# Cached attention decode with a gated feed-forward mix: per-slab normalization and output projection inside the K/V stream, a fourth K slot, and a longer lead of K over V

## Chip, cores, metric

One core of one Trainium2 chip. The metric is device microseconds of one execution. A *span* is the profiled execution from first to last instruction.

The *granted clock* (PEclk) is the share of its full clock at which TensorE ran, as the profile records it. Its values here are 0.5, called the half clock, and 1.0; figures between are means over a stretch.

Engines: TensorE (PE in the profile; its weight loads are PEld), VectorE (DVE), ScalarE (ACT), GpSimd (POOL), and SyncE (SP), which here issues most DMAs.

## The reference, cut to what matters

```python
x = A_x                                          # 2 x 1 x 512
g = sigmoid((x * gate_w).sum(-1, keepdims=True))
# A: decode attention, B=2 batches, 32 heads, 4096 cached keys, head size 128
q = (x @ wq)                                     # 512 -> 32*128
scores = einsum("bhqd,bhkd->bhqk", q, k) * 128 ** -0.5
o = einsum("bhqk,bhkd->bhqd", softmax(scores), v)
a = o.reshape(2, 1, 4096) @ wo                   # 4096 -> 512
# B: relu feed-forward 512 -> 1376 -> 512
b = relu(x @ w1) @ w2
return g * a + (1 - g) * b
```

There are 64 (batch, head) pairs, called slabs here. Each needs 1 MiB of K and 1 MiB of V. The two caches are 134 MB of the 146 MB that its DMAs move.

## The kernel before

SP queues loads into rings: three slots of K, five of V. V of slab t-2 is issued behind K of slab t; this distance is called the lag below. For each slab, TensorE transposes K in 32 blocks of 128x128. DVE and ACT copy the blocks out of PSUM. TensorE then makes the scores (32 matmuls of one column). A maximum over all partitions on POOL, an exponential on ACT and 32 one-column matmuls with V, together called pv, give the unnormalized output.

```python
RK, RV, RKT, NP, NS = 3, 5, 2, 3, 4
# SP
for t in range(NSLAB):
    dma_k(t)                     # waits until TensorE freed slot t % RK
    if t >= 2:
        dma_v(t - 2)             # waits until TensorE freed slot (t-2) % RV
    ...                          # weights at some t
dma_v(NSLAB - 2)
dma_v(NSLAB - 1)
# TensorE
for t in range(NITER):           # NSLAB + 3
    transposes of slab t, groups 0..3
    scores(t - 1)
    transposes of slab t, groups 4..7
    pv(t - 3)                    # unnormalized output, one column of psACC
    ...
```

Everything else of the attention waits for the last pv: the sums of exponentials, the division, the output projection, and the mix with the feed-forward part.

```python
# TensorE, after the loop
emit(psACC[:, ACC_SUMS:...], lhsT=ones_f, rhs=rowsum)         # sums over partitions
for n4 in range(NN4):            # 4
    for h in range(Hq):          # 32: 128 matmuls of 2 columns
        emit(psACC[:, ACC_AT + 2*n4:...], lhsT=wo_sb[:, h, n4*P:(n4+1)*P], rhs=o_sb[:, 2*h:2*h+2], ...)
for n4 in range(NN4):            # back to rows: 8 matmuls with the identity
    emit(psS[0][0:B, ...], lhsT=at_sb[...], rhs=ident)
    emit(psS[1][0:B, ...], lhsT=fT_sb[...], rhs=ident)
# DVE, after the loop: reciprocal 128x64, multiply 128x64, copy, then three operations of 2x512
```

## Time and profile before

| | before |
|---|---|
| time, median of the first 6 runs | 375.23 us (374.73 to 375.87) |
| span of the profiled execution | 373.9 us |
| DMA rate in mid stream | 412 to 415 GB/s at a busy share of 1.01 to 1.02 |
| TensorE busy | 302.1 us |
| last V load landed (trace of completions) | 362.56 us |
| from there to the end of the span | 11.3 us |

Lines of the profile page of the kernel before: TensorE's busy time; granted clock, DMA share and rate in 40 equal slices; the chain that ended last.

```profile
PE 302.1 (81%) x6502; PEld 297.6 (80%) x6502; DVE 193.7 (52%) x402; ACT 167.4 (45%) x386; POOL 23.3 (6%) x71
...
PEclk9997655765965676568865688565858588686665
DMA  8999999999999999999999999999999999999930
GB/s 293 402 367 406 408 417 419 418 418 421 410 405 421 416 419 399 416 419 415 416 401 407 401 420 409 405 422 403 400 422 418 418 420 415 410 402 420 421 135 2
...
DMA 58%; PE 39%; DVE 1%; issue 1%; ACTq 0%; DVEq 0%
```

DMA is at 9 tenths from the second slice to the 38th. TensorE is busy 81% and yet no limit. The next line is from its list of waits (engine, what it was about to do, what it waited for: us in total, times, longest): it still waits for K to land.

```profile
PE psT L344 <- DMA k_ring<-in_A_k_cache_dram: 46.3, 34, 4.6
```

The windows view gives each engine's busy time in chosen stretches, then granted clock, DMA share and GB/s. It shows a hole near the start:

```profile
core 0: us, PE busy (x) PEld busy (x) DVE busy (x) ACT busy (x) POOL busy (x), PEclk, DMA share, GB/s
20.00:22.00 2.00, 2.00 (x22) 2.00 (x20) 1.68 (x3) 1.29 (x3) 0.00 (x0) 1.00 1.07 369
22.00:24.00 2.00, 2.00 (x49) 2.00 (x48) 1.53 (x3) 1.61 (x3) 0.00 (x0) 1.00 0.90 238
24.00:26.00 2.00, 1.79 (x32) 1.58 (x29) 1.88 (x5) 1.37 (x5) 0.38 (x1) 1.00 1.01 426
...
183.00:330.00 147.00, 124.12 (x2640) 122.50 (x2638) 80.70 (x166) 71.40 (x166) 9.47 (x27) 0.69 1.01 412
```

Here is the timeline of the kernel before, from the last pv on (start us, length us, engine, line, operation, out<-in, shapes, count, idle time before it and its releaser):

```profile
362.69 0.99 PE L344 MATMUL psACC<-p_ring,v_ring 128*128 128x1 bf16 x32 [0.81 <-DMA v_ring<-in_A_v_cache_dram]
...
363.55 0.67 PE L344 MATMUL psACC<-rowsum,ones_f 128*128 128x64 f32 x2
364.25 0.56 DVE L322 RECIPROCAL rinv<-psACC 128x64 f32<-128x64 f32 x1 [3.86 <-PE psACC L344]
364.89 0.23 DVE L324 TENSOR_TENSOR o_sb<-psACC,rinv 128x64 bf16<-128x64 f32 x1
...
365.17 3.57 PE L344 MATMUL psACC<-o_sb,wo_sb 128*128 128x2 bf16 x128 [0.96 <-DVE o_sb L324]
368.78 0.17 DVE L328 CAST at_sb<-psACC 128x8 bf16<-128x8 f32 x1 [3.67 <-PE psACC L344]
...
370.05 0.68 DVE L330 COPY f_sb<-psS 2x512 f32<-2x512 f32 x1 [1.10 <-PE psS L344]
370.81 0.68 DVE L332 TENSOR_TENSOR diff_sb<-psS,f_sb 2x512 f32<-2x512 f32 x1
371.58 0.74 DVE L334 SCALAR_TENSOR_TENSOR fin_sb<-diff_sb,g_sb,f_sb 2x512 bf16<-2x512 f32 x1
372.34 0.31 SPq L183 DMA_DIRECT2D out_dram<-fin_sb  x1
```

Each step waits for the one above it, and no K or V moves any more. The last V was issued at 349.17 and landed 13.39 us later. These 11.3 us cannot overlap with the stream as the kernel stands.

### The profile page before, as it was taken

How to read it: one execution, taken by the hardware profiler on the slowest of the kernel's cores; microseconds unless marked ns; L12 is line 12 of the kernel's file. 1: busy time of each engine (PE TensorE's matmuls, PEld its weight loads, DVE VectorE, ACT ScalarE, POOL GpSimd, SP SyncE). 2: the span in 40 equal slices, each digit the busy share in tenths (PEclk: the TensorE clock that was granted, in tenths of full speed). 3: DMA queues.
4: the chain of work that ended last, by engine and by line, in shares of the span. 5: the costliest groups of instructions: out<-in, count | busy, mean ns of one | idle time of the engine just before them, and what ended most of it. 6: DMA issues, size and time to landing. Idle time of an engine off the chain costs nothing.

```text
span 373.9 us, 14183 instructions
## 1 busy us (share of the span) xinstructions
PE 302.1 (81%) x6502; PEld 297.6 (80%) x6502; DVE 193.7 (52%) x402; ACT 167.4 (45%) x386; POOL 23.3 (6%) x71
## 2 busy tenths in 40 slices
PE   0197879879859998799867988689898988897984
PEld 0197879879859998799867978689898988897974
DVE  0085345655645664466544656355656556465532
ACT  1064334544534554355443555354555455454520
POOL 0000000000000000000000000000000000000000
PEclk9997655765965676568865688565858588686665
DMA  8999999999999999999999999999999999999930
GB/s 293 402 367 406 408 417 419 418 418 421 410 405 421 416 419 399 416 419 415 416 401 407 401 420 409 405 422 403 400 422 418 418 420 415 410 402 420 421 135 2
DMA packets 26711, 146.34 MB, mean 391 GB/s; under 512 B 2230, under 2 KB 7708, under 8 KB 10268
## 3 DMA queue, kind: packets, MB, share of 16 engines
q1 hardware_dynamic: 25588, 142.98, 94.2%
q10 hardware_dynamic: 1064, 2.46, 1.7%
q8 instruction: 51, 0.84, 0.9%
q14 instruction: 8, 0.07, 0.0%
HBM read 145.43 MB, written 0.00 MB: 389 GB/s over the span
## 4 chain that ended last, share of the span: by engine, by line
DMA 58%; PE 39%; DVE 1%; issue 1%; ACTq 0%; DVEq 0%
DMA k_ring<-in_A_k_cache_dram 51%; PE psT L344 26%; PE psS L344 7%; PE psACC L344 5%; DMA wq_sb<-in_A_wq_dram 4%; DMA v_ring<-in_A_v_cache_dram 4%; PE psMISC L344 1%; DVE fin_sb L334 0%; DVE kt_ring L268 0%; DVE diff_sb L332 0%; DVE f_sb L330 0%; DVE rinv L322 0%; ACTq L190 0%; ACTq L192 0%; DVE o_sb L324 0%
## 5 line engine op out<-in xcount | busy, mean ns | idle before, releaser
L268 DVE CAST kt_ring<-psT 128x512 bf16<-128x512 f32 x256 | 172.8, 690 | 123.7 <-PE psT L344 121.7
L344 PE MATMUL psT<-ident,k_ring 128*128 128x128 bf16 x2048 | 198.5, 275 | 46.9 <-DMA k_ring<-in_A_k_cache_dram 46.3
L203 ACT CAST kt_ring<-psT 128x512 bf16<-128x512 f32 x256 | 145.4, 586 | 183.5 <-PE psT L344 182.6
L344 PEld LDWEIGHTS psT<-ident,k_ring 128*128 128x128 bf16 x2048 | 172.4, 127 | 50.2 <-DMA k_ring<-in_A_k_cache_dram 49.7
L344 PE MATMUL psACC<-p_ring,v_ring 128*128 128x1 bf16 x2048 | 63.5, 165 | 1.8 <-issue 1.0
L344 PEld LDWEIGHTS psACC<-p_ring,v_ring 128*128 128x128 bf16 x2048 | 62.7, 101 | 2.1 <-issue 2.0
L344 PE MATMUL psS<-qT_sb,kt_ring 128*128 128x1 bf16 x2048 | 64.0, 165 | 0.1
L344 PEld LDWEIGHTS psS<-qT_sb,kt_ring 128*128 128x128 bf16 x2048 | 63.7, 102 | 0.2
L240 POOL PARTITION_ALL_REDUCE allmax<-colmax x64 | 22.5, 351 | 324.4 <-DVE colmax L275 324.4
L275 DVE TENSOR_REDUCE colmax<-psS 128x1 f32<-128x32 f32 x64 | 12.3, 192 | 27.9 <-PE psS L344 27.9
L210 ACT ACTIVATE p_ring<-psS,negb 128x32 bf16<-128x32 f32 x64 | 18.6, 290 | 3.6 <-DVE negb L281 1.6
L210 ACT ACTIVATION_READ_ACCUMULATOR p_ring<-psS,negb 128x1 f32 x64 | 12.6, 198 | 0.0
L344 PE MATMUL psMISC<-ident,x_sb 2*128 2x2 bf16 x4 | 0.3, 165 | 13.4 <-POOL ident L234 13.4
L344 PEld LDWEIGHTS psMISC<-ident,x_sb 2*128 2x128 bf16 x4 | 0.2, 101 | 13.4 <-POOL ident L234 13.4
L281 DVE TENSOR_SCALAR negb<-allmax 128x1 f32<-128x1 f32 x64 | 9.2, 144 | 0.5 <-POOL allmax L240 0.5
L344 PE MATMUL psMISC<-xT_sb,wq_sb 128*128 128x2 bf16 x128 | 4.0, 165 | 3.7 <-DMA wq_sb<-in_A_wq_dram 3.7
L344 PEld LDWEIGHTS psMISC<-xT_sb,wq_sb 128*128 128x128 bf16 x128 | 3.7, 104 | 3.8 <-issue 3.8
L344 PEld LDWEIGHTS psACC<-o_sb,wo_sb 128*128 128x128 bf16 x128 | 3.5, 104 | 1.1 <-DVE o_sb L324 1.1
L344 PE MATMUL psACC<-o_sb,wo_sb 128*128 128x2 bf16 x128 | 3.6, 165 | 1.0 <-DVE o_sb L324 1.0
L248 DVE SCALAR_TENSOR_TENSOR gscr<-x_sb,gw_sb 2x512 f32<-2x512 bf16 x1 | 0.7, 680 | 6.8 <-DMA gw_sb<-in_gate_w_dram 6.8
L253 DVE CAST xT_sb<-psMISC 128x8 bf16<-128x8 f32 x1 | 0.2, 167 | 6.2 <-PE psMISC L344 6.2
L196 ACT ACT_TABLE_LOAD x1 | 1.3, 1283 | 3.1 <-issue 3.1
(32 smaller groups left out, 15.2 us busy)
## 6 DMA issues: line engine op xcount, KB each, us to landing
k_ring<-in_A_k_cache_dram SPq DMA_DIRECT2D x64, 1024.0 KB, 11.4
v_ring<-in_A_v_cache_dram SPq DMA_DIRECT2D x64, 1024.0 KB, 13.7
wo_sb<-in_A_wo_dram SPq DMA_DIRECT2D x4, 1024.0 KB, 15.8
wq_sb<-in_A_wq_dram SPq DMA_DIRECT2D x3, 1024.0 KB, 14.8
w_sb<-in_B_w_dram ACTq DMA_DIRECT2D x1, 1376.0 KB, 19.9
w_sb<-in_B_w_dram SPq DMA_DIRECT2D x1, 1280.0 KB, 20.4
wq_sb<-in_A_wq_dram ACTq DMA_DIRECT2D x1, 1024.0 KB, 15.3
w_sb<-in_B_w_dram SPq DMA_DIRECT2D x1, 96.0 KB, 21.0
```

The source lines that it names most:

```text
L196: nc.scalar.activation(out=gexp[:, :], in_=gdot[:, :], func=AF.Exp, scale=-1.0).then_inc(sem_gexp, 1)
L203: nc.scalar.copy(out=kt_ring[:, ks, 4 * g:4 * g + 4, :], in_=psT[b][:, :].rearrange("p (a d) -> p a d", d=P),).then_inc(sem_cp[b], 1)
L210: nc.scalar.activation(out=p_ring[:, u % NP, :], in_=psS[u % 2][:, 0:NCH], func=AF.Exp, bias=negb[:, u % NS:u % NS + 1], scale=SCALE, accu ...
L240: nc.gpsimd.partition_all_reduce(allmax[:, u % NS:u % NS + 1], colmax[:, u % NS:u % NS + 1], channels=P, reduce_op=RMAX,).then_inc(sem_all ...
L248: nc.vector.scalar_tensor_tensor(out=gscr[:, :], in0=x_sb[:, :], scalar=1.0, in1=gw_sb[:, :], op0=ALU.mult, op1=ALU.mult, accum_out=gdot[: ...
L253: nc.vector.tensor_copy(out=xT_sb[:, :], in_=psMISC[:, M_XT:M_XT + 2 * KT]).then_inc(sem_xTsb, 1)
L268: nc.vector.tensor_copy(out=kt_ring[:, ks, 4 * g:4 * g + 4, :], in_=psT[b][:, :].rearrange("p (a d) -> p a d", d=P),).then_inc(sem_cp[b], 1)
L275: nc.vector.tensor_reduce(out=colmax[:, u % NS:u % NS + 1], in_=psS[u % 2][:, 0:NCH], axis=AX.X, op=ALU.max).then_inc(sem_rmax, 1)
L281: nc.vector.tensor_scalar_mul(negb[:, u % NS:u % NS + 1], allmax[:, u % NS:u % NS + 1], -SCALE).then_inc(sem_negb, 1)
L344: mm = nc.tensor.matmul(out_ap, lhsT=lhsT, rhs=rhs, start=start, stop=stop)
```

## The change

The intent is to normalize and project each slab as soon as its pv is done, so that little is left at the end, and to prefetch K deeper. The projection of one head becomes a single matmul of 512 columns with a weight from `wo`, called a row or wo row below. The diff, cut and condensed to its core:

```diff
-    RK, RV, RKT, NP, NS = 3, 5, 2, 3, 4
+    RK, RV, RKT, NP, NS = 4, 5, 2, 3, 4
+    LV = 3
@@ SP
-                if t >= 2:
-                    dma_v(t - 2)
+                if t >= LV:
+                    dma_v(t - LV)
@@ POOL: a second all-reduce per slab, for the sum of exponentials
+            def do_sums(u):
+                pool.wait_ge(sem_exp, u + 1)
+                nc.gpsimd.partition_all_reduce(S_sb[:, ...], rowsum[:, ...], channels=P, reduce_op=RADD)
@@ DVE: per slab, after the row maximum
+                dve_recip(t - 3)          # 128x1
+                dve_norm(t - 4)           # o_sb column = psACC column * reciprocal
@@ TensorE: one row of the projection per slab of the second batch
+            def a_rows_mm(h):
+                emit(psEPI[0:B, 0:D], lhsT=o_sb[:, 2*h:2*h+2], rhs=wo_sb[:, h, :], start=(h == 0), stop=(h == Hq-1), ...)
@@ TensorE: the loop (NITER is now NSLAB + 4)
+                if t == 0:
+                    qT_piece(0)           # first q projection between the halves of slab 0's transposes
                 ...
                 pv(t - 3)                 # now also waits for the normalization of the slab before
+                h_a = t - 36
+                if 0 <= h_a < Hq:
+                    a_rows_mm(h_a)
@@ the feed-forward result is made as rows too (11 matmuls of 512 columns) and scaled by 1-g early
-                fT_mms()
+                f_rows_mms()
@@ after the loop: sums, 128 wo matmuls, identity matmuls and five DVE operations go; one DVE operation stays
```

More of the change, by code (lines that the diff above doesn't have):

```diff
@@ L17, in bass_gated_mix__gqa_block_cached__dense_activation_relu__decode_kernel @@
     RMAX = bass.bass_isa.ReduceOp.max
+    RADD = bass.bass_isa.ReduceOp.add
     B, _, D = A_x.shape
@@ L28, in bass_gated_mix__gqa_block_cached__dense_activation_relu__decode_kernel @@
     WLAST = Dff - NJF * P
-    NN4 = D // P
     SCALE = float(Dh) ** -0.5
     GROUPS = NCH // 4
-    RK, RV, RKT, NP, NS = 3, 5, 2, 3, 4
+    NTB = 4
+    RK, RV, RKT, NP, NS = 4, 5, 2, 3, 4
+    LV = 3
     QT_PIECES = 4
@@ L52, in bass_gated_mix__gqa_block_cached__dense_activation_relu__decode_kernel @@
         g_sb = ctx.enter_context(nc.sbuf_tensor("g_sb", [B, 1], f32))
+        omg = ctx.enter_context(nc.sbuf_tensor("omg", [B, 1], f32))
         ident = ctx.enter_context(nc.sbuf_tensor("ident", [P, P], bf16))
         itmp = ctx.enter_context(nc.sbuf_tensor("itmp", [P, P], bf16))
-        ones_f = ctx.enter_context(nc.sbuf_tensor("ones_f", [P, P], f32))
         xT_sb = ctx.enter_context(nc.sbuf_tensor("xT_sb", [P, 2 * KT], bf16))
         hT_sb = ctx.enter_context(nc.sbuf_tensor("hT_sb", [P, 2 * NJ], bf16))
-        fT_sb = ctx.enter_context(nc.sbuf_tensor("fT_sb", [P, 2 * NN4], bf16))
         qT_sb = ctx.enter_context(nc.sbuf_tensor("qT_sb", [P, 2 * Hq], bf16))
@@ L63, in bass_gated_mix__gqa_block_cached__dense_activation_relu__decode_kernel @@
         negb = ctx.enter_context(nc.sbuf_tensor("negb", [P, NS], f32))
+        S_sb = ctx.enter_context(nc.sbuf_tensor("S_sb", [P, NS], f32))
+        rS_sb = ctx.enter_context(nc.sbuf_tensor("rS_sb", [P, NS], f32))
         rowsum = ctx.enter_context(nc.sbuf_tensor("rowsum", [P, NSLAB], f32))
         o_sb = ctx.enter_context(nc.sbuf_tensor("o_sb", [P, NSLAB], bf16))
-        rinv = ctx.enter_context(nc.sbuf_tensor("rinv", [P, NSLAB], f32))
-        at_sb = ctx.enter_context(nc.sbuf_tensor("at_sb", [P, 2 * NN4], bf16))
         f_sb = ctx.enter_context(nc.sbuf_tensor("f_sb", [B, D], f32))
-        diff_sb = ctx.enter_context(nc.sbuf_tensor("diff_sb", [B, D], f32))
+        pre_sb = ctx.enter_context(nc.sbuf_tensor("pre_sb", [B, D], f32))
         fin_sb = ctx.enter_context(nc.sbuf_tensor("fin_sb", [B, D], bf16))
-        psT = [ctx.enter_context(nc.psum_tensor(f"psT{i}", [P, 512], f32)) for i in range(4)]
+        psT = [ctx.enter_context(nc.psum_tensor(f"psT{i}", [P, 512], f32)) for i in range(NTB)]
         psS = [ctx.enter_context(nc.psum_tensor(f"psS{i}", [P, 512], f32)) for i in range(2)]
@@ L75, in bass_gated_mix__gqa_block_cached__dense_activation_relu__decode_kernel @@
         psMISC = ctx.enter_context(nc.psum_tensor("psMISC", [P, 512], f32))
-        ACC_O, ACC_SUMS, ACC_AT = 0, NSLAB, 2 * NSLAB
-        M_QT, M_XT, M_HT, M_FT = 0, 2 * Hq, 2 * Hq + 2 * KT, 100
+        psEPI = psMISC
+        M_QT, M_XT, M_HT = 0, 2 * Hq, 2 * Hq + 2 * KT
         def sem(name):
@@ L99, in bass_gated_mix__gqa_block_cached__dense_activation_relu__decode_kernel @@
         sem_hTsb = sem("sem_hTsb")
-        sem_fT = sem("sem_fT")
-        sem_fTsb = sem("sem_fTsb")
-        sem_tr = [sem(f"sem_tr{i}") for i in range(4)]
-        sem_cp = [sem(f"sem_cp{i}") for i in range(4)]
+        sem_f = sem("sem_f")
+        sem_fsb = sem("sem_fsb")
+        sem_tr = [sem(f"sem_tr{i}") for i in range(NTB)]
+        sem_cp = [sem(f"sem_cp{i}") for i in range(NTB)]
         sem_scores = sem("sem_scores")
@@ L108, in bass_gated_mix__gqa_block_cached__dense_activation_relu__decode_kernel @@
         sem_exp = sem("sem_exp")
+        sem_S = sem("sem_S")
+        sem_pv = sem("sem_pv")
+        sem_onrm = sem("sem_onrm")
         sem_gdot = sem("sem_gdot")
         sem_gexp = sem("sem_gexp")
-        sem_sums = sem("sem_sums")
-        sem_onrm = sem("sem_onrm")
-        sem_AT = sem("sem_AT")
-        sem_ATsb = sem("sem_ATsb")
-        sem_rows = sem("sem_rows")
+        sem_A = sem("sem_A")
         sem_fin = sem("sem_fin")
@@ L124, in slab_col @@
             return 2 * h + b
-        NITER = NSLAB + 3
+        NITER = NSLAB + 4
         @block.sync
@@ L179, in _ @@
                     dma_wo_piece((t - 16) // 8)
-            dma_v(NSLAB - 2)
-            dma_v(NSLAB - 1)
+            for u in range(NSLAB - LV, NSLAB):
+                dma_v(u)
             sp.wait_ge(sem_fin, 1)
@@ L184, in _, with group_info @@
             sp.wait_ge(sem_out, 16)
+        def group_info(t, g):
+            G = GROUPS * t + g
+            bank = G % NTB
+            k = G // NTB
+            return bank, k
         @block.scalar
@@ L199, in act_copy @@
                 ks = t % RKT
-                b = g % 4
-                n = 2 * t + g // 4 + 1
-                act.wait_ge(sem_tr[b], n)
+                bank, k = group_info(t, g)
+                act.wait_ge(sem_tr[bank], k + 1)
                 nc.scalar.copy(
                     out=kt_ring[:, ks, 4 * g:4 * g + 4, :],
-                    in_=psT[b][:, :].rearrange("p (a d) -> p a d", d=P),
-                ).then_inc(sem_cp[b], 1)
+                    in_=psT[bank][:, :].rearrange("p (a d) -> p a d", d=P),
+                ).then_inc(sem_cp[bank], 1)
             def act_exp(u):
@@ L231, in _ @@
             pool.memset(itmp[:, :], 1.0)
-            pool.memset(ones_f[:, :], 1.0)
             pool.drain()
@@ L237, in _, with do_allmax @@
             ).then_inc(sem_ident, 1)
-            for u in range(NSLAB):
+            def do_allmax(u):
                 pool.wait_ge(sem_rmax, u + 1)
@@ L242, in _ @@
                 ).then_inc(sem_allred, 1)
+            def do_sums(u):
+                pool.wait_ge(sem_exp, u + 1)
+                nc.gpsimd.partition_all_reduce(
+                    S_sb[:, u % NS:u % NS + 1], rowsum[:, slab_col(u):slab_col(u) + 1], channels=P, reduce_op=RADD,
+                ).then_inc(sem_S, 1)
+            for u in range(NSLAB):
+                do_allmax(u)
+                if u >= 1:
+                    do_sums(u - 1)
+            do_sums(NSLAB - 1)
         @block.vector
@@ L253, in _ @@
             nc.vector.tensor_copy(out=xT_sb[:, :], in_=psMISC[:, M_XT:M_XT + 2 * KT]).then_inc(sem_xTsb, 1)
-            dve.wait_ge(sem_qT, 1)
-            nc.vector.tensor_copy(
-                out=qT_sb[:, 0:2 * HEADS_PER_PIECE], in_=psMISC[:, M_QT:M_QT + 2 * HEADS_PER_PIECE]
-            ).then_inc(sem_qTsb, 1)
             dve.wait_ge(sem_gexp, 1)
@@ L261, in _ @@
             dve.reciprocal(g_sb[:, :], g1[:, :])
+            dve.drain()
+            dve.tensor_scalar(omg[:, :], g_sb[:, :], -1.0, 1.0, ALU.mult, ALU.add)
             def dve_copy(t, g):
                 ks = t % RKT
-                b = g % 4
-                n = 2 * t + g // 4 + 1
-                dve.wait_ge(sem_tr[b], n)
+                bank, k = group_info(t, g)
+                dve.wait_ge(sem_tr[bank], k + 1)
                 nc.vector.tensor_copy(
                     out=kt_ring[:, ks, 4 * g:4 * g + 4, :],
-                    in_=psT[b][:, :].rearrange("p (a d) -> p a d", d=P),
-                ).then_inc(sem_cp[b], 1)
+                    in_=psT[bank][:, :].rearrange("p (a d) -> p a d", d=P),
+                ).then_inc(sem_cp[bank], 1)
             def dve_reduce_max(u):
@@ L283, in dve_negb, with dve_recip, dve_norm @@
                 ).then_inc(sem_negb, 1)
+            def dve_recip(u):
+                dve.wait_ge(sem_S, u + 1)
+                dve.reciprocal(rS_sb[:, u % NS:u % NS + 1], S_sb[:, u % NS:u % NS + 1])
+            def dve_norm(u):
+                col = slab_col(u)
+                dve.wait_ge(sem_pv, u + 1)
+                nc.vector.tensor_tensor(
+                    out=o_sb[:, col:col + 1], in0=psACC[:, col:col + 1], in1=rS_sb[:, u % NS:u % NS + 1],
+                    op=ALU.mult,
+                ).then_inc(sem_onrm, 1)
             def dve_qT_copy(pz):
@@ L299, in _ @@
                     dve_reduce_max(u)
+                if t == 0:
+                    dve_qT_copy(0)
+                ur = t - 3
+                if 0 <= ur < NSLAB:
+                    dve_recip(ur)
+                un = t - 4
+                if 0 <= un < NSLAB:
+                    dve_norm(un)
                 if t < NSLAB:
@@ L311, in _ @@
                 if t == 5:
-                    dve.wait_ge(sem_fT, 1)
-                    nc.vector.tensor_copy(out=fT_sb[:, :], in_=psMISC[:, M_FT:M_FT + 2 * NN4]).then_inc(sem_fTsb, 1)
+                    dve.wait_ge(sem_f, 1)
+                    nc.vector.tensor_copy(out=f_sb[:, :], in_=psEPI[0:B, 0:D]).then_inc(sem_fsb, 1)
+                    dve.drain()
+                    dve.tensor_scalar_mul(pre_sb[:, :], f_sb[:, :], omg[:, 0:1])
                 if t == 7:
@@ L319, in _ @@
                     dve_qT_copy(3)
-            dve.wait_ge(sem_sums, 1)
-            dve.reciprocal(rinv[:, :], psACC[:, ACC_SUMS:ACC_SUMS + NSLAB])
-            dve.drain()
-            nc.vector.tensor_tensor(
-                out=o_sb[:, :], in0=psACC[:, ACC_O:ACC_O + NSLAB], in1=rinv[:, :], op=ALU.mult
-            ).then_inc(sem_onrm, 1)
-            dve.wait_ge(sem_AT, 1)
-            nc.vector.tensor_copy(out=at_sb[:, :], in_=psACC[:, ACC_AT:ACC_AT + 2 * NN4]).then_inc(sem_ATsb, 1)
-            dve.wait_ge(sem_rows, 1)
-            dve.tensor_copy(out=f_sb[:, :], in_=psS[1][0:B, 0:D])
-            dve.drain()
-            dve.tensor_tensor(out=diff_sb[:, :], in0=psS[0][0:B, 0:D], in1=f_sb[:, :], op=ALU.subtract)
-            dve.drain()
+            dve.wait_ge(sem_A, 1)
             nc.vector.scalar_tensor_tensor(
-                out=fin_sb[:, :], in0=diff_sb[:, :], scalar=g_sb[:, 0:1], in1=f_sb[:, :],
+                out=fin_sb[:, :], in0=psEPI[0:B, 0:D], scalar=g_sb[:, 0:1], in1=pre_sb[:, :],
                 op0=ALU.mult, op1=ALU.add,
@@ L360, in qT_piece @@
                 pe.wait_ge(sem_wq[pz], 16)
+                if pz == 0:
+                    pe.wait_ge(sem_xTsb, 1)
                 for hh in range(HEADS_PER_PIECE):
@@ L368, in qT_piece @@
                              inc=(sem_qT, 1) if last else None)
-            pe.wait_ge(sem_xTsb, 1)
-            qT_piece(0)
             def transposes(t, g):
-                b, h = slabs[t]
                 ks_in = t % RK
-                bank = g % 4
-                n = 2 * t + g // 4
-                if n > 0:
-                    pe.wait_ge(sem_cp[bank], n)
+                bank, k = group_info(t, g)
+                if k > 0:
+                    pe.wait_ge(sem_cp[bank], k)
                 for i in range(4):
@@ L394, in scores @@
                 if explicit_cp_wait:
-                    for bank in range(4):
-                        pe.wait_ge(sem_cp[bank], 2 * u + 2)
+                    need = [0] * NTB
+                    for g in range(GROUPS):
+                        bank, k = group_info(u, g)
+                        need[bank] = max(need[bank], k + 1)
+                    for bank in range(NTB):
+                        if need[bank] > 0:
+                            pe.wait_ge(sem_cp[bank], need[bank])
                 for c in range(NCH):
@@ L405, in pv @@
                 pe.wait_ge(sem_exp, u + 1)
+                if u >= 1:
+                    pe.wait_ge(sem_onrm, u)
                 pe.wait_ge(sem_v[vs], 16 * (u // RV + 1))
                 for c in range(NCH):
-                    emit(psACC[:, ACC_O + col:ACC_O + col + 1],
+                    emit(psACC[:, col:col + 1],
                          lhsT=v_ring[:, vs, c, :], rhs=p_ring[:, u % NP, c:c + 1],
                          start=(c == 0), stop=(c == NCH - 1),
-                         inc=(sem_vfree[vs], 1) if c == NCH - 1 else None)
+                         inc=(sem_pv, 1) if c == NCH - 1 else None)
+                pending.append((sem_vfree[vs], 1))
             def hT_mms():
@@ L423, in hT_mms, with f_rows_mms @@
                              inc=(sem_hT, 1) if last else None)
-            def fT_mms():
+            def f_rows_mms():
                 pe.wait_ge(sem_w2, 32)
                 pe.wait_ge(sem_hTsb, 1)
-                for n4 in range(NN4):
-                    for j in range(NJ):
-                        w = P if j < NJF else WLAST
-                        last = (n4 == NN4 - 1) and (j == NJ - 1)
-                        emit(psMISC[:, M_FT + 2 * n4:M_FT + 2 * n4 + 2],
-                             lhsT=w2_sb[0:w, j, n4 * P:(n4 + 1) * P], rhs=hT_sb[0:w, 2 * j:2 * j + 2],
-                             start=(j == 0), stop=(j == NJ - 1),
-                             inc=(sem_fT, 1) if last else None)
+                for j in range(NJ):
+                    w = P if j < NJF else WLAST
+                    emit(psEPI[0:B, 0:D],
+                         lhsT=hT_sb[0:w, 2 * j:2 * j + 2], rhs=w2_sb[0:w, j, :],
+                         start=(j == 0), stop=(j == NJ - 1),
+                         inc=(sem_f, 1) if j == NJ - 1 else None)
+            def a_rows_mm(h):
+                pe.wait_ge(sem_onrm, Hkv + h + 1)
+                if h == 0:
+                    pe.wait_ge(sem_fsb, 1)
+                    pe.wait_ge(sem_qTsb, 4)
+                if h % HEADS_PER_PIECE == 0:
+                    pe.wait_ge(sem_wo[h // HEADS_PER_PIECE], 16)
+                emit(psEPI[0:B, 0:D], lhsT=o_sb[:, 2 * h:2 * h + 2], rhs=wo_sb[:, h, :],
+                     start=(h == 0), stop=(h == Hq - 1),
+                     inc=(sem_A, 1) if h == Hq - 1 else None)
             for t in range(NITER):
@@ L444, in _ @@
                     scores(u, explicit_cp_wait=(t >= NSLAB))
+                if t == 0:
+                    qT_piece(0)
                 if t < NSLAB:
@@ L454, in _ @@
                 if t == 4:
-                    fT_mms()
+                    f_rows_mms()
                 if t == 6:
-                    pe.wait_ge(sem_fTsb, 1)
+                    pe.wait_ge(sem_fsb, 1)
                     qT_piece(1)
@@ L464, in _ @@
                     qT_piece(3)
-            pe.wait_ge(sem_exp, NSLAB)
-            emit(psACC[:, ACC_SUMS:ACC_SUMS + NSLAB], lhsT=ones_f[:, :], rhs=rowsum[:, :],
-                 start=True, stop=True, inc=(sem_sums, 1))
-            pe.wait_ge(sem_onrm, 1)
-            for pz in range(QT_PIECES):
-                pe.wait_ge(sem_wo[pz], 16)
-            for n4 in range(NN4):
-                for h in range(Hq):
-                    last = (n4 == NN4 - 1) and (h == Hq - 1)
-                    emit(psACC[:, ACC_AT + 2 * n4:ACC_AT + 2 * n4 + 2],
-                         lhsT=wo_sb[:, h, n4 * P:(n4 + 1) * P], rhs=o_sb[:, 2 * h:2 * h + 2],
-                         start=(h == 0), stop=(h == Hq - 1),
-                         inc=(sem_AT, 1) if last else None)
-            pe.wait_ge(sem_ATsb, 1)
-            pe.wait_ge(sem_fTsb, 1)
-            for n4 in range(NN4):
-                emit(psS[0][0:B, n4 * P:(n4 + 1) * P],
-                     lhsT=at_sb[:, 2 * n4:2 * n4 + 2], rhs=ident[:, :], start=True, stop=True)
-                emit(psS[1][0:B, n4 * P:(n4 + 1) * P],
-                     lhsT=fT_sb[:, 2 * n4:2 * n4 + 2], rhs=ident[:, :], start=True, stop=True,
-                     inc=(sem_rows, 1) if n4 == NN4 - 1 else None)
             assert not pending
```

## The prediction

> **What bounds the kernel now.** DMA. The windows view shows a DMA share of 1.01 to 1.02 and 412 to 415 GB/s from 34 to 352 us; the page's chain gives DMA 58%. TensorE is second: 302.1 us busy of 373.9, and in the list of waits it still waits 46.3 us for k_ring landings, so it keeps up. The stream cannot be shortened by doing less on the engines: bytes and packets are the same before and after.
>
> **Where time is to be had: the two ends.** In the timeline the last V slab was issued at 349.17 and landed 13.39 us later, at 362.56. From there to the end, 11.3 us, nothing streams: pv(63) 0.99, the ones-by-rowsum matmuls 0.67, reciprocal 0.56 and multiply 0.23 on 128x64, 128 wo matmuls 3.57, a cast 0.17, eight identity matmuls about 1, three 2x512 DVE operations of 0.68, 0.68 and 0.74, and about 1.55 from the end of the last one to the end of the span.
>
> **Tail after.** Sums, reciprocals, all but one normalization and all but two wo rows lie inside the stream. From the landing of V63: 0.1 start, pv(63) 1.0, then the wo row of head 30 runs while norm(63) (estimate 0.15, as the cast of 128x8 took 0.17) is done, then head 31's. A 512-column row is estimated from the identity matmuls (16 of 128 columns took 1.89 us at granted clock 0.5): 0.45 us, 0.6 to its end. Final operation 0.74, output 1.55. Sum 4.3 to 4.5 us instead of 11.3: saves 6.9.
>
> **Head.** K3 waited for the release of ring slot 0 until 21.98 us; between 22.5 and 24.0 us the stream fell to 174 to 240 GB/s. With four K slots K3, V0 and the next wq piece are queued before that wait. I estimate 0.3 MB, 0.5 us, gained. Half of the first transposes move ahead of the q projection; that shortens TensorE only.
>
> **What is added, and hidden.** DVE: 64 reciprocals and 64 multiplies, 0.13 to 0.17 each as the 128x1 negb's 0.144, so +18 us to about 212 of 368. POOL: 64 more all-reduces at 0.35 (if add costs as max). TensorE: 32 rows of 512 columns, 8 to 15 us, minus about 5 removed; only in the second half, where the windows view has it 84% busy. Deeper K prefetch covers bursts. The Trainium skill, "TensorE: Matmul & The Clock Gate", Part 1, says that activity releases the half clock; the trace's clock does switch between 0.5 and 1.0 only, so more work should raise the mean (0.699) rather than starve the stream. The later V (lag 3) still lands before its pv: about 2.5 us after its K, with 3 us of work between.
>
> **Sum.** 375.2 - 6.9 - 0.5 = 367.8 us, range 366.0 to 370.2. Faster by over 2% means below 367.7, so it is nearly even: faster 0.48, within 2% 0.50, slower 0.02.
>
> **Signs.** Right if V63 lands at 361.5 to 362.6, 4 to 5 us before the end; no DMA dip at 22.5 to 24; k_ring waits remain, though fewer.
>
> **What would make it wrong.** TensorE falling behind in the second half (k_ring waits vanish); the add all-reduce taking microseconds; drain of uneven DMA engines (205 GB/s from 357 to 360) growing or shrinking.

## The result

The changed kernel takes 368.12 us (median of 8 runs, 367.61 to 368.73). The kernel before takes 375.25 us (16 runs, 374.56 to 375.91). The ratio is 0.981, with a 95% interval from 0.980 to 0.982. Ratios in this document divide the mean of one kernel's fast runs by that of the other's of the same rounds, so they are not quite the ratios of the medians.

The same views of the changed kernel follow. First, its page:

```profile
PE 308.7 (84%) x6363; PEld 291.6 (80%) x6363; DVE 198.6 (54%) x527; ACT 167.3 (46%) x386; POOL 46.1 (13%) x134
...
PEclk9996756766655886558875885559677688595885
DMA  8999999999999999999999999999999999999971
GB/s 297 390 390 412 409 417 416 420 418 421 407 409 421 419 415 398 420 418 417 419 391 419 421 417 410 390 421 421 416 421 419 417 419 416 421 419 419 419 310 66
...
DMA 70%; PE 26%; SPq 2%; issue 1%; DVE 0%; ACTq 0%
...
L251 POOL PARTITION_ALL_REDUCE S_sb<-rowsum x64 | 29.2, 456 | 0.3 <-ACT p_ring L215 0.3
...
L368 PE MATMUL psMISC<-wo_sb,o_sb 128*2 128x512 bf16 x32 | 14.4, 457 | 0.0
```

TensorE's wait for K, and the windows:

```profile
PE psT L368 <- DMA k_ring<-in_A_k_cache_dram: 36.9, 29, 4.2
```

```profile
20.00:22.00 2.00, 1.80 (x30) 1.58 (x28) 1.48 (x3) 1.07 (x2) 0.11 (x1) 1.00 1.11 394
22.00:24.00 2.00, 2.00 (x52) 1.79 (x50) 1.70 (x5) 1.50 (x5) 0.42 (x2) 1.00 0.99 401
24.00:26.00 2.00, 2.00 (x62) 2.00 (x60) 1.22 (x4) 1.33 (x4) 0.57 (x2) 1.00 0.97 397
...
183.00:330.00 147.00, 130.30 (x2681) 121.92 (x2677) 83.66 (x223) 71.49 (x167) 19.82 (x56) 0.72 1.02 415
```

The timeline from the last pv on:

```profile
361.92 0.99 PE L368 MATMUL psACC<-p_ring,v_ring 128*128 128x1 bf16 x32 [0.69 <-DMA v_ring<-in_A_v_cache_dram]
...
362.84 1.01 PE L368 MATMUL psMISC<-wo_sb,o_sb 128*2 128x512 bf16 x2
362.95 0.16 DVE L306 TENSOR_TENSOR o_sb<-psACC,rS_sb 128x1 bf16<-128x1 f32 x1 [2.04 <-PE psACC L368]
...
363.89 0.74 DVE L358 SCALAR_TENSOR_TENSOR fin_sb<-psMISC,g_sb,pre_sb 2x512 bf16<-2x512 f32 x1 [0.78 <-PE psMISC L368]
364.65 0.32 SPq L183 DMA_DIRECT2D out_dram<-fin_sb  x1
```

The last V landed at 361.78 us and the span ended at 366.2. The tail is 4.43 us instead of 11.33, which saves 6.9. The last landing is 0.8 us earlier, and the hole at 22 us is gone (401 GB/s instead of 238). Together that is 7.7 us between the two profiled executions. The medians differ by 7.1, because the two profiled executions lie on opposite sides of their medians.

In mid stream almost nothing changed: from 183 to 330 us the share of DMA is 1.01 before and 1.02 after, at 412 and 415 GB/s.

### The profile page after: what moved, and what is told of

It is laid out like the page before. It is cut to its first block, busy times and chain, and to the rows that moved or that the text cites. A ratio compares the mean times of both kernels' runs of the same rounds, so it can differ in the third digit from the quotient of the medians.

```text
span 366.2 us, 14094 instructions
## 1 busy us (share of the span) xinstructions
PE 308.7 (84%) x6363; PEld 291.6 (80%) x6363; DVE 198.6 (54%) x527; ACT 167.3 (46%) x386; POOL 46.1 (13%) x134
## 4 chain that ended last, share of the span: by engine, by line
DMA 70%; PE 26%; SPq 2%; issue 1%; DVE 0%; ACTq 0%
DMA k_ring<-in_A_k_cache_dram 62%; PE psT L368 18%; PE psS L368 5%; DMA v_ring<-in_A_v_cache_dram 4%; DMA wq_sb<-in_A_wq_dram 3%; PE psACC L368 2%; PE psMISC L368 2%; SPq L151 1%; SPq L134 0%; DVE fin_sb L358 0%; DVE kt_ring L282 0%; SPq L161 0%; ACTq L196 0%; ACTq L198 0%; ACTq L197 0%
## 5 line engine op out<-in xcount | busy, mean ns | idle before, releaser
L368 PE MATMUL psT<-ident,k_ring 128*128 128x128 bf16 x2048 | 194.7, 272 | 37.5 <-DMA k_ring<-in_A_k_cache_dram 36.9
L368 PEld LDWEIGHTS psT<-ident,k_ring 128*128 128x128 bf16 x2048 | 168.2, 125 | 49.0 <-DMA k_ring<-in_A_k_cache_dram 43.8
L251 POOL PARTITION_ALL_REDUCE S_sb<-rowsum x64 | 29.2, 456 | 0.3 <-ACT p_ring L215 0.3
L368 PE MATMUL psMISC<-wo_sb,o_sb 128*2 128x512 bf16 x32 | 14.4, 457 | 0.0
L306 DVE TENSOR_TENSOR o_sb<-psACC,rS_sb 128x1 bf16<-128x1 f32 x64 | 9.2, 143 | 4.0 <-PE psACC L368 4.0
L301 DVE RECIPROCAL rS_sb<-S_sb 128x1 f32<-128x1 f32 x64 | 9.8, 153 | 0.4 <-POOL S_sb L251 0.4
```

The source lines that it names most:

```text
L251: nc.gpsimd.partition_all_reduce(S_sb[:, u % NS:u % NS + 1], rowsum[:, slab_col(u):slab_col(u) + 1], channels=P, reduce_op=RADD,).then_inc ...
L301: dve.reciprocal(rS_sb[:, u % NS:u % NS + 1], S_sb[:, u % NS:u % NS + 1])
L306: nc.vector.tensor_tensor(out=o_sb[:, col:col + 1], in0=psACC[:, col:col + 1], in1=rS_sb[:, u % NS:u % NS + 1], op=ALU.mult,).then_inc(sem ...
L368: mm = nc.tensor.matmul(out_ap, lhsT=lhsT, rhs=rhs, start=start, stop=stop)
```

## Experiments

Two theories stood at the start. The first is the prediction's: the shortened end gives nearly all, and the ring only fills the hole at the head. The rival is that the deeper ring feeds the stream and is worth several microseconds. Twelve kernels ran. Every result was correct. The table is ordered by what was asked. "Gap" is the time from the landing of the last K to that of the last V, and "tail" the time from there to the end of the span. Both are read from the trace's record of completed loads in one profiled execution.

| run | median us (range) | ratio to before | gap us | tail us |
|---|---|---|---|---|
| before | 375.25 (374.56 to 375.91) | | 8.81 | 11.33 |
| changed | 368.12 (367.61 to 368.73) | 0.981 | 10.77 | 4.43 |
| e1 ring and lag alone, on the kernel before | 374.70 (374.60 to 375.08) | 0.9984 | 11.41 | 11.33 |
| e2 ring and lag undone | 369.90 (369.14 to 371.89) | 0.9867 | 7.42 | 9.72 |
| e3 head order undone | 368.26 (368.06 to 368.40) | 0.9811 | 11.17 | 4.43 |
| e7 ring 3, lag 3 | 368.21 (367.76 to 371.43) | 0.9827 | 11.08 | 4.65 |
| e8 ring 4, lag 2 | 369.70 (367.88 to 374.73) | 0.9847 | 7.54 | 8.51 |
| e4 all wo rows at the end | 376.20 (375.29 to 376.83) | 1.0019 | 11.00 | 13.20 |
| e6 wo rows doubled | 368.89 (368.77 to 369.02) | 0.9832 | 10.93 | 5.28 |
| e11 e2 with rows doubled | 369.90 (369.23 to 372.70) | 0.9861 | 8.27 | 6.73 |
| e9 last V split, row first | 367.75 (367.17 to 367.99) | 0.9798 | 10.93 | 4.59 |
| e10 e9 with spare rows | 369.58 (368.92 to 371.21) | 0.9849 | 11.10 | 7.47 |
| e12 e9 with row order mended | 368.10 (367.20 to 370.16) | 0.9819 | 11.11 | 3.89 |
| e5 loads moved between DMA engines | 441.81 (438.42 to 446.30) | 1.1735 | | |

The ranges of e5 and e8 include runs called slow: two of e5, above 446 us, and one of e8, 374.73 us, each over 1.5% above the fastest of its kernel. The ratios leave them out. The 95% intervals of the ratios reach 0.001 to 0.002 to each side, for e2, e7, e8, e11 and e12 0.002 to 0.003, and for e5 0.004.

### e1: the ring and the lag alone, on the kernel before

```diff
-    RK, RV, RKT, NP, NS = 3, 5, 2, 3, 4
+    RK, RV, RKT, NP, NS = 4, 5, 2, 3, 4
-                if t >= 2:
-                    dma_v(t - 2)
+                if t >= 3:
+                    dma_v(t - 3)
```

> The kernel before with four K slots and V issued three slabs behind K, nothing else changed. Theory (the epilogue gives nearly all, the ring only fills the dip at 22 us): 0.3 to 1.0 us faster than before, so 374.3 to 375.0 us, the last V landing at most 1 us earlier, tail after it still 11.3 us. Rival (the deeper ring feeds the stream and is worth several us): 372 us or less.

It took 374.70 us against 375.27 in the same rounds, 0.57 us faster. The tail is unchanged at 11.33 us, and the windows view from 22 to 24 us gives 401 GB/s. So the ring and lag together are worth about half a microsecond on the old kernel. The rival is out.

### e2: the ring and the lag undone in the changed kernel

```diff
-    RK, RV, RKT, NP, NS = 4, 5, 2, 3, 4
-    LV = 3
+    RK, RV, RKT, NP, NS = 3, 5, 2, 3, 4
+    LV = 2
```

> The changed kernel with three K slots and V two slabs behind, as before the change. Theory: loses only the 0.3 to 1.0 us of the head, 368.4 to 369.1 us, tail after the last landing still 4.4 us. Rival (the ring is worth several us): 371 us or more.

Neither theory fits. It lost 1.8 us by the medians, and its runs scatter. In its profiled execution, one of the two slowest at 371.89 us, the last V landed at 360.44 us, earlier than in the changed kernel, but the tail was 9.72 us. The windows view of that run:

```profile
340.00:345.00 5.00, 5.00 (x93) 4.55 (x92) 2.74 (x8) 2.62 (x6) 0.71 (x2) 0.50 1.01 421
345.00:350.00 5.00, 5.00 (x96) 4.95 (x94) 3.15 (x8) 2.60 (x6) 0.71 (x2) 0.50 1.02 421
350.00:355.00 5.00, 5.00 (x77) 4.60 (x77) 2.93 (x7) 1.90 (x5) 0.71 (x2) 0.50 1.01 415
355.00:360.00 5.00, 5.00 (x88) 4.55 (x86) 2.58 (x8) 2.16 (x6) 0.71 (x2) 0.50 0.57 236
```

TensorE is busy 5.00 of every 5.00 us, at granted clock 0.50. Its timeline shows the first transposes of the last slab and the last pv:

```profile
356.13 1.89 PE L368 MATMUL psT<-ident,k_ring 128*128 128x128 bf16 x16
...
365.84 1.01 PE L368 MATMUL psACC<-p_ring,v_ring 128*128 128x1 bf16 x32
```

K of that slab had landed at 353.02 us. TensorE came to it 3.1 us late, then needed 10.7 us (356.13 to 366.85) for all that lies behind the last K. The last V had been in place for 5 us when its product began. So in this run TensorE set the end, not DMA.

### e3: the order at the head undone

```diff
+            qT_piece(0)
             for t in range(NITER):
 ...
-                if t == 0:
-                    qT_piece(0)
```

> The changed kernel with the first q projection ahead of all transposes again. Theory: TensorE is not the limit in the head, so the same within 0.3 us, 367.8 to 368.5 us. Rival (starting the transposes earlier releases slot 0 earlier and is part of the gain): 0.5 us or more slower.

It took 368.26 us with the same tail of 4.43 us. Moving the first q projection behind half of the transposes is worth nothing that these runs resolve.

### e7 and e8: which of ring and lag

e7 sets `RK` to 3 and keeps `LV` at 3. e8 keeps `RK` at 4 and sets `LV` to 2.

> The changed kernel with three K slots but V still three slabs behind K. Undoing both slots and lag cost 1.8 us, more than the head explains; in that trace TensorE was busy without a gap from 340 us on at granted clock 0.50 and finished behind the stream. Lag theory (with lag 3 the last K has four V loads behind it instead of three, so TensorE gets 2.5 us more for its last slabs): within 0.6 us of the changed kernel, 367.8 to 368.7 us. Ring theory (the fourth slot lets K run ahead of a slow TensorE): 369.3 us or more.

> The changed kernel with four K slots but V two slabs behind K. Lag theory: 369.3 us or more, the last V landing earlier than TensorE is ready for it. Ring theory: within 0.6 us of the changed kernel, 367.8 to 368.7 us.

e7 is level with the changed kernel by its median (368.21 us). The intervals of the two ratios overlap (0.9803 to 0.9852 against 0.980 to 0.982), so no cost of the missing fourth slot is shown. e8 is as late as e2 (369.70), and its runs scatter as widely. It differs from the changed kernel in the lag alone, and its interval (0.9826 to 0.9869) lies apart. So the lag costs time, and the number of slots is not shown to. (Set against each other, the intervals of e7 and e8 overlap.) The table's gaps show why. With lag 2, three V loads follow the last K, and the last V lands 7.4 to 8.8 us after it. With lag 3 there are four, and the gap is 10.8 to 11.4 us. Behind the last K, TensorE has its slab, the scores of two slabs, four more pv and the last rows to do. Where the gap is shorter than that work, the last V waits for TensorE. The timeline of e8's profiled execution (370.72 us) shows the first transposes of the last slab and the last pv:

```profile
355.76 1.07 PE L368 MATMUL psT<-ident,k_ring 128*128 128x128 bf16 x16
...
364.67 1.01 PE L368 MATMUL psACC<-p_ring,v_ring 128*128 128x1 bf16 x32
```

That stretch is 8.9 us, more than the gap of 7.54, although the granted clock was 1.00 from 350 to 360 us (0.57 in the mean from 360 to 365). TensorE had also come to the last K 2.8 us after its landing (352.94). Both together make the last pv 4.2 us late (the last V landed at 360.48). One of e7's six runs took 371.43 us. No trace shows why, but lag 3 is no assurance that every execution is in time.

On the old kernel the gap of 8.81 us was just enough: its last pv had waited 0.81 us for V. The change put rows and waits into that stretch, and also lengthened the stretch.

### e4: all wo rows behind the loop

```diff
-                h_a = t - 36
-                if 0 <= h_a < Hq:
-                    a_rows_mm(h_a)
 ...
+            for h in range(Hq):
+                a_rows_mm(h)
```

> The changed kernel with all 32 wo rows behind the loop instead of one per slab. Theory (the gain is that the projection is hidden, not that it is cheaper): 30 more rows of 0.43 us at the half clock after the last landing, about 12.5 us more, 379 to 381 us, slower than before the change. If the clock rises while they run, 0.22 us each from some point on: 375 to 379. Rival (the row form itself is cheaper than 128 narrow matmuls): 371 us or less.

It took 376.20 us, so the whole gain was gone. The timeline of the end:

```profile
362.76 9.79 PE L368 MATMUL psMISC<-wo_sb,o_sb 128*2 128x512 bf16 x32
...
372.59 0.74 DVE L358 SCALAR_TENSOR_TENSOR fin_sb<-psMISC,g_sb,pre_sb 2x512 bf16<-2x512 f32 x1 [9.56 <-PE psMISC L368]
```

The row form takes 9.79 us for what 128 narrow matmuls did in 3.57. It pays only because 30 of its 32 rows hide behind DMA. My first figure, 379 to 381 us, was too high because the granted clock rose while the rows ran: it was 0.50 up to 366 us and 1.00 from 369 us on. The second alternative held.

### e6: every wo row computed twice

```diff
-                     start=(h == 0), stop=(h == Hq - 1), inc=...)
+                     start=(h == 0), stop=False)
+                emit(psEPI[0:B, 0:D], lhsT=o_sb[:, 2*h:2*h+2], rhs=wo_sb[:, h, :], start=False, stop=(h == Hq - 1), inc=...)
 ...
-                out=fin_sb[:, :], in0=psEPI[0:B, 0:D], scalar=g_sb[:, 0:1], ...
+                out=fin_sb[:, :], in0=psEPI[0:B, 0:D], scalar=gh_sb[:, 0:1], ...   # gh = g / 2
```

> The changed kernel with every wo row computed twice into the same sum and the gate halved, so the result is right; adds 14.4 us of TensorE work to the second half and one row, 0.43 us, to the end. Prediction's view (ample slack in TensorE): 368.3 to 368.8 us. Thin slack (0.45 us per slab on top of 84% busy plus the first row leaves nothing at the half clock): 369.5 to 373 us, and the last V waits for TensorE.

It took 368.89 us, 0.77 more than the changed kernel. That is 0.09 us above the range of the prediction's view, and well below that of thin slack. The tail grew by 0.85 us (5.28 against 4.43), since two rows more lie in it, so the tail accounts for all of it. The 30 rows in the stream cost nothing. This line of its page shows what happened:

```profile
PE 302.3 (82%) x6395; PEld 276.3 (75%) x6395; DVE 196.0 (53%) x528; ACT 166.6 (45%) x386; POOL 46.1 (13%) x134
```

TensorE did more work and was busy for less time, 302.3 us instead of 308.7. Its mean granted clock was 0.79 instead of 0.72 in the profiled executions. The Trainium skill, "TensorE: Matmul & The Clock Gate", Part 1, says that the default state is the half clock and that activity releases it. This pair of runs agrees in direction. e2 does not fit so simply: there TensorE had no gap for 20 us and stayed at 0.50.

### e11: does a higher clock cure e2?

This is e2 with the rows doubled as in e6.

> Three K slots and lag 2 as in the run with the ring undone (369.9 us), and every wo row doubled as in the doubled-row run (368.9 us with ring and lag in place). Clock theory (the ring undone is slow because TensorE ends the stream at the half clock, and more work lifts the clock): 368.7 to 369.3 us, faster than with less work, and a narrower range than 369.1 to 371.9. Work theory (TensorE is late because there is too much to do): 371 us or more.

It took 369.90 us, the same as e2, so both theories missed. In the profiled execution the clock was up:

```profile
340.00:345.00 5.00, 4.09 (x106) 3.57 (x102) 2.91 (x9) 2.55 (x7) 0.71 (x2) 1.00 1.02 423
345.00:350.00 5.00, 4.12 (x107) 3.59 (x104) 2.94 (x9) 2.58 (x7) 0.71 (x2) 1.00 1.02 423
350.00:355.00 5.00, 4.09 (x106) 3.57 (x103) 2.91 (x9) 2.56 (x7) 0.71 (x2) 1.00 0.93 387
```

TensorE had gaps and met the last K as it landed, at 353.34 us. Its last pv still began at 363.17, 1.6 us after the last V (361.60). Even with the clock mostly up, then, the work behind the last K, with its doubled rows, took longer than the gap of 8.3 us. How much of e2's lateness is due to its slow clock is not separated by this, because the doubled rows also add work behind the last K. But e8 was late with no doubled rows and with the clock at 1.00 for the ten us before 360. What e2, e8 and e11 share is the short gap. In e2 and e8, over half of the lateness was there when the last K landed (3.1 and 2.8 us): TensorE still had work of earlier slabs to do.

### e9, e12, e10: can the remaining tail be cut?

e9 cuts the last V load into four by chunks, with a semaphore each, and puts each wo row ahead of the slab's pv:

```diff
+            for i in range(NPC):                      # 4
+                sp.dma_start(v_ring[:, s, c0:c1, :], src[:, c0:c1, :]).then_inc(sem_vlast[i], 16)
 ...
+                    if u == NSLAB - 1 and c % (NCH // NPC) == 0:
+                        pe.wait_ge(sem_vlast[c // (NCH // NPC)], 16)
```

> The changed kernel with the last V load cut into four by chunks, each with its own semaphore, so that three quarters of the last product run before the last landing, and with the wo row of a slab put ahead of that slab's product instead of behind it. Theory (the 4.4 us after the last landing are a chain of which the product, 1.0 us, and the row of head 30, about 0.2 us beyond the normalization, can be taken out): 0.7 to 1.0 us faster, 367.1 to 367.4 us. Rival (smaller packets on the slow DMA engines delay the landing by as much): within 0.3 us of 368.1.

It took 367.75 us, with a ratio to before of 0.9798 (0.9784 to 0.9811). That lies between the two ranges. It is 0.37 us less than the changed kernel, and the intervals overlap, so it is not shown to be better. In its trace the last pv began at 362.06 us, later than the last landing at 361.68. The order may be the reason, since a row ahead of a pv waited about 0.25 us for the normalization just before it. e12 asks whether it is.

e12 keeps the split and puts the rows behind their pv again, all but the row of head 30.

> The last V load cut into four as in the split run, but each wo row behind its product again, as in the changed kernel, except the row of head 30, which goes ahead of the last product. In the split run three rows each waited 0.25 us for the normalization just before them and the last product began 0.4 us after the last landing (362.06 against 361.68). Theory: TensorE is in time again, 367.0 to 367.5 us, at or below the split run's 367.75. Rival (TensorE is late for other reasons): 367.7 us or more.

The profiled execution had the shortest span of all that were profiled, 365.6 us with a tail of 3.89. But the six runs spread from 367.20 to 370.16 us, and their median, 368.10, lies in the rival's range. The gain is there in an execution where TensorE is in time, and it does not come reliably. So the order of the rows is not the whole reason.

e10 adds to e9 useless matmuls of the size of a wo row, into partitions of PSUM that nobody reads: one per slab, and eight between the last V landings.

> The kernel with the last V split, plus useless matmuls of one wo row each into an unread corner of PSUM: one per slab beside the real row, eight in the last gaps between V landings. In the doubled-row run extra TensorE work raised the granted clock from 0.72 to 0.79 and cost nothing but its share of the tail; in the split run TensorE reached the last product late, at clock 0.50, 0.4 us after the landing. Theory (work that keeps the clock up makes TensorE early at the end): 367.0 to 367.4 us, mean clock 0.77 or more. Rival (the spare rows only fill TensorE): 368 us or more.

It was slower, 369.58 us, in the rival's range. The mean granted clock of its runs was 0.714 to 0.752, against e6's 0.748 to 0.794. In its profiled execution, the slowest of the four (371.21 us), the tail was 7.47 us. Its timeline:

```profile
360.73 1.87 PE L378 MATMUL psMISC<-wo_sb,o_sb 128*2 128x512 bf16 x5
...
363.47 1.87 PE L378 MATMUL psMISC<-wo_sb,o_sb 128*2 128x512 bf16 x5
365.27 1.01 PE L378 MATMUL psACC<-p_ring,v_ring 128*128 128x1 bf16 x32
```

The granted clock was 0.50 from 345 to 365 us, and the eight spare rows found no gaps. They stand ahead of the last two pv, and the last one began 3.3 us after the last landing (362.00). Two rows cost 0.85 us in e6's tail, so eight come to 3.4 us, an estimate that accounts for all of this. Useless work is not a reliable way to a higher clock. Why these matmuls lifted it less than the doubled rows of e6, which have the same shape, stays open.

### e5: loads moved from the slow to the fast DMA engines

The trace records the 16 partial completions of each load, one per DMA engine. For the last V of the changed kernel, eight come between 351.8 and 355.2 us and eight between 360.0 and 361.8. The distance between the two groups grows through the run, in their means from 0.4 us at the first K to 7.7 at the last V. In the kernel before it ends smaller, 355.9 to 358.0 and 360.7 to 362.6, and in e7 the means end 2.0 us apart. If half of the engines finish 8 us early, moving some partitions to them should help.

```diff
+        def k_parts(t):
+            if t % 5 == 2:
+                return [(0, 112), (112, 120), (120, 128)]
+            return [(0, 128)]
```

> The changed kernel, 13 of the 64 K loads split by partitions 112 + 8 + 8[...]. Reason: in both traces the 16 partial completions of one load split into two groups of 8 whose distance grows through the run, to 7 us for the last V[...]. If the faster group is the 8 lowest engines, the end moves by about 3.5 us, to 364 to 366 us, and the spread of the last load's completions falls below 4 us. If the faster group is the highest, it is 3 to 4 us slower, 371 to 372. If the groups are mixed over the numbers, within 1.5 us of 368.1.

The 8 lowest engines stand here for the ones that take the small pieces. The traces name no engine, so that is a supposition. For the last V the medians of the two groups lie 8.0 us apart in the changed kernel and 4.9 in the kernel before, not 7 in both.

All three expectations failed. It took 441.81 us (440.24 by the four fast runs). After each of the 13 split loads the stream fell to half its rate for some 7 us; the windows view around one of them:

```profile
82.00:84.00 2.00, 1.77 (x49) 1.78 (x50) 1.29 (x2) 1.07 (x2) 0.00 (x0) 0.96 1.04 229
84.00:86.00 2.00, 1.81 (x19) 1.54 (x16) 1.58 (x5) 0.74 (x2) 0.71 (x2) 0.50 0.95 209
86.00:88.00 2.00, 0.99 (x32) 0.94 (x32) 0.18 (x2) 0.71 (x3) 0.00 (x0) 0.50 1.03 217
88.00:90.00 2.00, 0.00 (x0) 0.00 (x0) 0.00 (x0) 0.00 (x0) 0.00 (x0) 0.50 0.99 238
```

The engines are busy (share 0.95 to 1.04) but move half. Of the 16,384 packets of 8 KB, 2,478 took over 500 ns, against 86 in the changed kernel. A likely reason is in the Trainium skill. "DMA: Bandwidth & Descriptors", section "The descriptor swizzle", says that in a load of 128 partitions each engine writes one SBUF port, and "SBUF — State Buffer", section "Door 1: The DMA port swizzle", gives the map of partitions to ports. A load of 112 partitions, or of 8, need not keep engines on ports of their own. No run here tests that, so it is argued and not shown. Which eight engines are the fast ones stays open too.

## Why the prediction was right

The prediction said 367.8 us, in a range of 366.0 to 370.2, and put the chances of a gain over 2% at nearly even. The result is 368.12 us, a gain of 1.9%. Point by point:

- **DMA bounds the stream, and only the ends can give time.** Right. The mid-stream rate is 412 and 415 GB/s, and e1, which changes only the stream, moves the time by 0.57 us.
- **Tail 4.3 to 4.5 us instead of 11.3.** Right, 4.43. The parts hold as well: pv 0.99, the normalization 0.16, two rows to their end 1.01, the last operation 0.74. e4 shows that hiding the projection is what pays.
- **Head 0.5 us.** Right in size. The last V landed 0.8 us earlier in the profiled execution, and e1 gives 0.57 us by its medians. The hole at 22 us is filled, and K of slab 3 is issued at 10.65 us instead of 21.98, as foreseen. But the fourth slot is not needed for that: from 22 to 24 us e7, with three slots, moved 414 GB/s, and e2, with neither slot nor lag, 377. In e2 the transposes that moved ahead of the q projection freed slot 0 earlier (K of slab 3 was issued at 19.76 us). So "that shortens TensorE only" was wrong for the hole. That the moved q projection adds nothing to the time agrees with e3.
- **TensorE has slack enough.** Right for the kernel as changed: waits for K remain, 36.9 us instead of 46.3. Its reason was wrong. "Deeper K prefetch covers bursts" names the fourth slot; e7 shows that it is worth nothing by the median, and e8 and e2 that without the third slab of V lag the kernel loses 1.6 to 1.8 us. Three V loads behind the last K leave TensorE 7.4 to 8.3 us; four leave about 11. I had treated the lag only as a risk (V arriving late for its pv). It is what keeps TensorE in time for the last V. That the change brought it along was luck: the same reasoning, asked for lag 2, gave 368.4 to 369.1 us for e2 and missed.
- **More work raises the mean clock.** The mean went from 0.699 to 0.719, and to 0.79 with the rows doubled, in the profiled executions. But e2 stayed at 0.50 while busy without a gap, and e10 gained little (0.714 to 0.752), so this is not a rule to build on.
- **Costs of the added work.** The add all-reduce took 456 ns at POOL against 351 for the maximum, not the same, and harmless. The 64 reciprocals and 64 multiplies have about 19 us of durations (153 and 143 ns each), as estimated. But DVE's busy time rose only from 193.7 to 198.6 us: operations overlap in the record (their durations alone add up to 203.5 and 221.1 us), and the old end went away. TensorE's rows took 14.4 us, within 8 to 15.

## What to carry to other kernels

Work behind the last load is paid in full, while the same work inside a stream that DMA bounds can be free, even in a form nearly three times as expensive (9.79 us against 3.57). Before moving it there, count what lies between the landing of the last input that needs much work and the landing of the last input of all. The order of the last few loads decides whether the engine reaches the end in time, and here it mattered more than the depth of the ring. A median hides such lateness, so look at the scatter of the runs and at what the last product waited for.

## What the Trainium skill lacked or had wrong

- "TensorE: Matmul & The Clock Gate", Part 1: it says that activity releases the half clock after a busy window of about 3.4 us. In e2 TensorE showed 20.00 us busy in 20 us at granted clock 0.50, so busy time in the profile is not the activity that counts. These runs do not show what is. The doubled rows (mean clock 0.79) lifted it; the spare rows of the same shape did so less (0.714 to 0.752).
- "DMA: Bandwidth & Descriptors", section "Latency and other measured facts": it says that engines 7 and 15 are usually slower, with a guessed cause that concerns DMAs issued from GpSimd. Here, with loads issued from SP, eight of the 16 completions of a load fall behind the other eight, so that at the last load the means of the two groups lie about 5 us apart (before), 8 us (changed) and 2 us (e7), in a stream of 350 us. No page has that.
- The same page gives the mapping of engines to partitions for 128 partitions only. Splitting 13 loads into 112, 8 and 8 partitions cost about 72 us (fast runs); no page has a figure for such a split.
- No page has the cost of the all-reduce over partitions on POOL, 351 ns for a maximum and 456 ns for a sum of 128x1 values here (POOL spans are rough).
